# Issuing the stores of sorted weight tiles from ScalarE's queue, and splitting one row exchange into three pieces, in a fused attention and Fourier-mix kernel

## The chip, the cores and the metric

The kernel runs on one core of a Trainium2 chip. The metric is the device time of one execution in microseconds, and the time quoted for a kernel is the median of its runs. The engines named below are TensorE (PE; its weight loads are PEld), VectorE (DVE), ScalarE (ACT), GpSimd (POOL) and SyncE (SP). SP computes nothing here: it issues DMA transfers, one after the other, and before each it waits for the semaphores that the transfer depends on.

## The reference

Two blocks are fused. The first is attention with a threshold, for 8 batches of 8 heads, 576 tokens and 64 columns a head; the second mixes tokens by a two-dimensional Fourier transform and ends in a two-layer network with a normalised input. Everything is float32.

```python
scores = (1/sqrt(D)) * matmul(q, k.transpose(0, 1, 3, 2))       # (8, 8, 576, 576)
scores = where(scores >= max(scores, -1, keepdims=True) - tau, scores, -1e9)
attn   = exp(scores - max(scores, -1)); attn = attn / (sum(attn, -1) + 1e-9)
x = matmul(attn, v)  ->  rearranged to (8, 576, 512)
u = x + real(fft(fft(x, axis=1), axis=2))
un = (u - mean(u)) / sqrt(var(u) + 1e-6)
out = u + relu(un @ w_ch1) @ w_ch2                              # w_ch1: 512x2048, w_ch2: 2048x512
```

## The kernel before

**Tiling.** Attention is done for two heads at a time (a pair, number `n`), four pairs a batch, 32 pairs in all. A pair takes five steps `t` of 128 query rows (the fifth takes the last 64 rows of both heads), so there are 160 steps, numbered `i`. In the loop from L1764 one iteration of `i` holds: the scores of step `i` (`scores`, L439), the maximum (L518, DVE), the exponential (L524, ACT) and the threshold (L528, ACT) in `softmax_first`; mask and sum (L539, DVE), the reciprocal (L546, DVE) in `softmax_second`; the division (L552, ACT, two instructions for the two heads) in `softmax_third`; and, one step behind, the transposition of the finished weights of step `i - 1`, because the product with V (`values_in_parts`, L730, PE) needs keys on the partitions.

**Two ways to transpose.** In most steps PE transposes the weights (L633, L641) and ACT copies them to `et_all`. In 40 steps, eight in each of the batches 3 to 7 (counted from 0), `decide` (L571) sends them another way: DVE transposes 32x32 blocks of `e` into a buffer `et_room` (L601, in `blocks`), SP stores that buffer to DRAM (L602, `e_blocks`, 576 KB), and in a later iteration SP loads it back in four pieces so that the blocks land in their places in `et_all` (L611, `fetch`). There is a single `et_room`, in an unused part of the first weight matrix, so a transposition must wait until the store of the one before it has landed. There are three buffers `e_blocks` in DRAM.

**The network beside it.** Groups of 512 tokens go through the two-layer network as a generator that yields after every block of matmuls; `fill()` takes as many blocks from it as an evenly spread budget allows and puts them between the pieces of an attention step. From the second group on (`two_level`) products are formed by a scheme with fewer multiplications: first-stage blocks at L1288 (PE), whose results are copied by ACT (L1297 to L1306) or added by DVE (L1225) and passed through Relu by ACT (L1230), then second-stage blocks at L1437 (PE). The first stage is the `phase[0] == 1` in which `decide` chooses DVE for the transposition. The coefficients of both stages come from DRAM through a ring of five buffers (`ensure`, L1161, SP), four loads ahead.

**Folding rows.** After the last value product of a pair, `fold_rows` adds and subtracts mirrored halves of its result `x` (L792, L797; POOL for all but the last pair of a batch). Pairs of odd number need the first rows of their two heads exchanged first: `swap_rows` copies the two rows to a small tile `swap` (L759, two DMAs) and back to each other's place (L763, two DMAs, which wait for the first two). For the first pair of a batch, `x` was held in another buffer, so `fold_rows` first copies it (L779, POOL) and then calls `swap_rows`. `fold_rows` is a generator, too: a piece of it runs at each call of `fold_more`, that is at `t > 2` in the loop and at the `background()` calls in the network's blocks; what is left at step `t == 1` of the next pair is run there at once.

**Order.** The program's order on each engine is that in which the Python code emits the instructions. SP's queue therefore holds, in one line: the loads of q, k (L140) and v (L158, L161), the ring's loads (L1161), the row exchanges, the stores of `e_blocks`, the loads of `et_all` and the stores of the result (L984). ACT issues five DMAs at the very start and none afterwards.

Of the kernel before, what the change touches and what calls it, by code (L numbers as in the profile page):

```python
# [18 lines left out]
def _reversed(ap):  # L19

    n = ap.shape[1]
    return bass.AP(
        tensor=ap.tensor,
        offset=ap.offset + n - 1,
        ap=[list(ap.ap[0]), [-1, n]],
    )
# [11 lines left out]
def _stepped(ap, start, step, n):  # L38

    return bass.AP(  # L40
        tensor=ap.tensor,
        offset=ap.offset + start,
        ap=[list(ap.ap[0]), [step, n]],
    )
# [3 lines left out]
def kernel(  # L48
# [12 lines left out]
    nc = tc.nc  # L61
# [112 lines left out]
    for u in range(2):  # L174
# [14 lines left out]
        out=q_scale[:], in0=tau_t[:], scalar1=0.0, scalar2=SCALE, op0=ALU.is_ge, op1=ALU.mult  # L189
# [3 lines left out]
        out=below[:], in0=tau_t[:], scalar1=0.0, scalar2=-3.0e38, op0=ALU.is_lt, op1=ALU.mult  # L193
# [3 lines left out]
        out=tau_pos[:], in0=tau_t[:], scalar1=0.0, scalar2=-1.0, op0=ALU.max, op1=ALU.mult  # L197
# [71 lines left out]
    et_room = w1[2][:, HID // 2 : HID // 2 + 4 * 9 * 32]  # L269
# [159 lines left out]
    def scores(i):  # L429
        n, t = divmod(i, NT)  # L430
        qT, kT = heads[n][0:2]

        nh = 2 if t < 4 else 1
        sc = [ps.tile([128, 2, 512], FP32, tag="sc", name=f"sc{j}") for j in range(nh)]
        if t < 4:
            for c in range(2):
                for j in range(2):
                    hp, k0 = slice(64 * j, 64 * j + 64), D * (1 - j)
                    nc.tensor.matmul(  # L439
                        sc[j][:, c, 0:HALF], qT[hp, 128 * t : 128 * t + 128],  # L440
                        kT[hp, k0 + HALF * c : k0 + HALF * (c + 1)], start=True, stop=True,
                    )
        else:
            for c in range(2):
                nc.tensor.matmul(
                    sc[0][:, c, 0:HALF], q_ends[:, :], kT[:, D + HALF * c : D + HALF * (c + 1)],
                    start=True, stop=True,
                )
        steps[i] = (sc, nh)
# [99 lines left out]
    def softmax_third(i):  # L549
        nh, e, den = steps[i]  # L550
        for j in range(nh):
            nc.scalar.activation(  # L552
                out=e[:, S * j : S * (j + 1)], in_=e[:, S * j : S * (j + 1)], func=ACT.Copy,
                scale=den[:, j : j + 1],
            )
        if nh == 1:
            nc.scalar.copy(e[:, S : S + 64], e[:, 512:S])
        steps[i] = (e, None)

    by_dma = {}  # L560
# [32 lines left out]
    scratch = [dram.tile([128, SLOT], FP32, name=f"e_blocks{u}") for u in range(3)]  # L593

    def blocks(i):

        if not by_dma[i]:
            return
        e = steps.pop(i)[0]
        out_ = et_room.rearrange("p (b c q) -> p c b q", b=4, c=NC9)  # L600
        nc.vector.transpose(out_, e[:, 0 : 2 * S])  # L601
        nc.sync.dma_start(out=scratch[i % 3][:, :], in_=et_room)  # L602

    def fetch(i):

# [146 lines left out]
    def swap_rows(n, later=False):  # L752
        b, p = n // NPAIR, PAIRS[n % NPAIR]
        x = xs[b][p]
        if p % 2:

            swap = sb.tile([2, S], FP32, tag="half", bufs=1, name="swap")
            for j in range(2):
                nc.sync.dma_start(out=swap[j : j + 1, :], in_=x[64 * j : 64 * j + 1, :])  # L759

            def back():
                for j in range(2):
                    nc.sync.dma_start(out=x[64 * j : 64 * j + 1, :], in_=swap[1 - j : 2 - j, :])  # L763

            if late and later:
                swaps.append(back)
            else:
                back()

# [4 lines left out]
    def fold_rows(n):  # L774
        b, p = n // NPAIR, PAIRS[n % NPAIR]
        if late and n % NPAIR == 0:
            assert not mixes
            x = sb.tile([128, S], FP32, tag=f"x{p}", bufs=1, name=f"x{p}")
            nc.gpsimd.tensor_copy(x[:, :], xs[b][p][:, :])  # L779
            xs[b][p] = x  # L780
            swap_rows(n)
            yield
        x = xs[b][p]

        half = sb.tile([128, 2, HALF], FP32, tag="half", bufs=1, name="half")
        up, down = x[:, 1:HALF], _reversed(x[:, HALF + 1 : S])
        mid = S // 4

        last = n % NPAIR == NPAIR - 1
        eng = nc.vector if last else nc.gpsimd  # L790
        for c, op in enumerate((ALU.add, ALU.subtract)):
            eng.tensor_tensor(out=half[:, c, 1:HALF], in0=up, in1=down, op=op)  # L792
        yield
        for c, c0, op in (
            (0, 0, ALU.add), (0, 161, ALU.subtract), (1, FW, ALU.subtract), (1, FW + 161, ALU.add)
        ):
            eng.tensor_tensor(  # L797
                out=f[:, p, c0 : c0 + mid - 1], in0=half[:, c, 1:mid],
                in1=_reversed(half[:, c, mid + 1 : HALF]), op=op,
            )  # L800
            if late and last and c0 > 0 and c0 != FW:
                yield

        eng.tensor_tensor(
            out=f[:, p, mid - 1 : mid + 1], in0=_stepped(x, mid, -mid, 2),
            in1=_stepped(x, 3 * mid, -mid, 2), op=ALU.add,
        )
        eng.tensor_tensor(
            out=_stepped(f[:, p, :], 160, FW, 2), in0=_stepped(x, 0, mid, 2),
            in1=_stepped(x, HALF, mid, 2), op=ALU.subtract,  # L810
        )
        yield


        if n % NPAIR == 1 and b != 1:
            fold_halves(b)

    def fold_halves(b):
        sums[b] = sb.tile([128, 2, 2 * FW], FP32, tag="tmp", bufs=1, name="sums")
        fold_chunks(nc.gpsimd, b, 1)  # L820
# [692 lines left out]
    late = []  # L1513
# [28 lines left out]
    total = B * per_batch  # L1542
# [117 lines left out]
    def fold_more():  # L1660
        if folds and next(folds[0], True):
            folds.pop(0)
# [101 lines left out]
    for i in range(2 * per_batch, total + 3):  # L1764


        n, t = divmod(i, NT)
        values = iter(())
        if i < total:
            scores(i)  # L1770
        late_values = None
        if t == 3 and i < total and not by_dma.get(i - 2):
            values = values_in_parts(n, 0)
        elif t == 0 and by_dma.get(i - 4):
            values = values_in_parts(n - 1, 0)
        elif t == 1 and n > 0:
            while folds:
                fold_more()
            values = values_in_parts(n - 1, 1)
            if by_dma.get(i - 3):  # L1780
                values, late_values = iter(()), values
        next(values, None)
        if i < total:
            softmax_first(i)
        next(values, None)
        if t == 0 and by_dma.get(i - 4):
            fetch(i - 3)
        if t != 4 or not by_dma.get(i - 3):
            fetch(i - 2)
        if i % per_batch == 2:  # L1790
            for _ in last_fold:
                pass
            start_batch(i // per_batch - 1)
        fill(True)
        for _ in late_values or ():
            pass
        if i < total:
            softmax_second(i)
        while held:
            held.pop(0)()  # L1800
        decide(i - 1)
        blocks(i - 1)
        while swaps:
            swaps.pop(0)()
        if mixes:
            mix(1)
        if t == 1:
            if n % NPAIR:
                folds.append(fold_rows(n - 1))
            else:  # L1810
                last_fold = fold_rows(n - 1)
                next(last_fold)
        weights = weights_in_parts(i - 1) if i <= total else iter(())
        next(weights, None)
        if t > 2:
            fold_more()
        fill()
        if i % per_batch == 1:
            next(last_fold)
        next(weights, None)  # L1820
        if i < total:
            softmax_third(i)
            if t == 1:
                prep_ends(n)
            if t == 2 and n + 1 < B * NPAIR:
                scale_q(n + 1)
            if t == 3 and n + 1 < B * NPAIR:
                prep_pair(n + 1)
        if wanted:
            wanted.pop().factors()  # L1830
        if i % per_batch == 1:
            next(last_fold)
        fill()
        if t == 2 and n + 1 < B * NPAIR:
            load_v(n + 1)
        if t < 2 and n + 1 < B * NPAIR and len(loaded.get(n + 1, ())) == t:
            load_raw(n + 1, slice(t, t + 1))
# [50 lines left out]
```

## Time and profile before

| | us |
|---|---|
| median of 3 runs (lowest to highest) | 1633.84 (1628.51 to 1636.37) |
| the profiled execution | 1636.11 |
| its span in the trace | 1634.0 |
| PE busy | 1523.9 (93%) |
| DVE busy | 1130.0 (69%) |
| ACT busy | 904.9 (55%) |
| POOL busy | 813.3 (50%) |

A profile shows one execution. Busy time counts instructions of an engine, not its waiting for semaphores nor the issuing of DMAs. The list of waits puts each idle stretch down to the instruction or transfer whose end came last before it. In timelines a row holds the start and the time of one instruction or of several alike, and in square brackets the idle time of the engine before it with what ended it; "SPq" rows are DMA issues, whose time is that of the issue alone, not of the transfer.

### The profile page before, as it was taken

The page shows a single profiled execution, that of the slowest core. Times are in us where ns is not written, and L with a number is a line of the kernel's source. Part 1 is how long each engine was busy: PE and PEld are TensorE (multiplying, and loading weights), DVE is VectorE, ACT ScalarE, POOL GpSimd, SP SyncE. Part 2 cuts the span into 40 slices and gives each one's busy share as a digit, 9 for nine tenths or more (in the row PEclk, how much of TensorE's full clock was granted, in tenths as well). Part 3 has the DMA queues.
Part 4 walks back from the last instruction along what each step waited for, and adds up shares of the span by engine and source line. Part 5 has one row for each costly group of instructions (what it writes and reads, how often), then busy time and mean ns, then how long its engine had stood idle before and what let it go on. Part 6 is the DMA issues. An engine that isn't in the chain of part 4 may idle for free.

```text
span 1634.0 us, 27080 instructions
## 1 busy us (share of the span) xinstructions
PE 1523.9 (93%) x9410; PEld 1166.9 (71%) x9410; DVE 1130.0 (69%) x2137; ACT 904.9 (55%) x1913; POOL 813.3 (50%) x1002
## 2 busy tenths in 40 slices
PE   8998989999999989998999899998999899999997
PEld 4555545556787867876787677776787678889987
DVE  7997786846769567766677577856677666636537
ACT  5775565545666556655666566665566566233231
POOL 6784663034454623536253724553264625547646
PEclk9999999999999999999999999999999999999998
DMA  7423221645945389737975588628974696556755
GB/s 159 125 56 113 74 74 36 190 144 177 285 149 165 94 253 261 203 97 203 248 203 143 141 252 244 187 79 230 255 205 127 178 264 203 186 160 230 238 188 191
DMA packets 296253, 286.26 MB, mean 175 GB/s; under 512 B 202643, under 2 KB 241045, under 8 KB 295222
## 3 DMA queue, kind: packets, MB, share of 16 engines
q1 hardware_dynamic: 293606, 284.23, 60.6%
q8 instruction: 76, 1.25, 0.3%
q10 hardware_dynamic: 2512, 0.30, 0.2%
q14 instruction: 59, 0.48, 0.1%
HBM read 231.10 MB, written 53.22 MB: 174 GB/s over the span
## 4 chain that ended last, share of the span: by engine, by line
PE 60%; DVE 19%; DMA 6%; ACT 6%; issue 4%; POOL 2%; SPq 2%; DVEq 0%; ACTq 0%; POOLq 0%
PE ph L1288 16%; PE po L1437 15%; PE pv L730 8%; PE sc L439 6%; PE po L1015 4%; PE ph L991 2%; DMA v_in<-in_v_dram 2%; PE pw L641 2%; DVE e L479 2%; PE py L864 2%; DMA w<-f 2%; PE pw L694 2%; ACT e L524 1%; DVE e L539 1%; DVE neg L518 1%
## 5 line engine op out<-in xcount | busy, mean ns | idle before, releaser
L518 DVE TENSOR_REDUCE neg<-sc 128x1 f32<-128x576 f32 x216 | 153.8, 749 | 127.0 <-PE sc L439 117.0
L524 ACT ACTIVATE e<-sc,neg 128x576 f32<-128x576 f32 x216 | 158.4, 733 | 136.5 <-DVE neg L518 135.8
L1437 PE MATMUL po<-w,w_all 128*128 128x128 f32 x1792 | 229.6, 278 | 1.2 <-ACT et_all L634 0.8
L1437 PEld LDWEIGHTS po<-w,w_all 128*128 128x128 f32 x1792 | 214.6, 193 | 11.0 <-issue 6.2
L1234 POOL TENSOR_TENSOR w<-hs 128x512 f32<-128x512 f32 x32 | 42.1, 1318 | 352.0 <-ACT hs L1230 325.3
L539 DVE SCALAR_TENSOR_TENSOR e<-sc,thr,e 128x576 f32<-128x576 f32 x216 | 168.4, 813 | 47.4 <-ACT thr L528 47.4
L1288 PE MATMUL ph<-w_all,w 128*128 128x256 f32 x672 | 168.9, 401 | 33.4 <-DVE hs L1225 33.4
L1288 PE MATMUL ph<-u_t,w 128*128 128x256 f32 x768 | 183.1, 383 | 0.0
L439 PE MATMUL sc<-kT,qT 64*128 64x288 f32 x1024 | 171.2, 434 | 9.4 <-DVE e L479 8.1
L1288 PEld LDWEIGHTS ph<-w_all,w 128*128 128x128 f32 x672 | 130.9, 199 | 65.1 <-POOL w_all L1337 23.6
L552 ACT ACTIVATE e<-e,den 128x576 f32<-128x576 f32 x216 | 156.8, 770 | 25.3 <-DVE den L546 24.9
L1288 PEld LDWEIGHTS ph<-u_t,w 128*128 128x128 f32 x768 | 142.3, 190 | 29.9 <-issue 9.0
L439 PEld LDWEIGHTS sc<-kT,qT 64*128 64x128 f32 x1024 | 94.2, 187 | 64.3 <-issue 35.7
L1230 ACT ACTIVATE hs<-hs 128x512 f32<-128x512 f32 x64 | 54.0, 843 | 152.6 <-DVE hs L1225 152.6
L1337 POOL TENSOR_TENSOR w_all<-w_all 128x128 f32<-128x128 f32 (+2 forms) x160 | 119.6, 765 | 33.0 <-DVE w_all L1455 22.4
L1437 PE MATMUL po<-w,hs 128*128 128x128 f32 x960 | 126.3, 279 | 0.0
L1437 PEld LDWEIGHTS po<-w,hs 128*128 128x128 f32 x960 | 117.3, 194 | 9.1 <-issue 7.7
L1225 DVE TENSOR_TENSOR hs<-ph,hs 128x512 f32<-128x512 f32 x64 | 60.5, 945 | 84.1 <-PE ph L1288 78.8
L730 PE MATMUL pv<-et_all,v_rev 128*64 128x256 f32 (+1 forms) x640 | 86.2, 416 | 4.3 <-DMA out_dram<-u 2.6
L730 PE MATMUL pv<-et_all,v_in 128*64 128x256 f32 (+1 forms) x640 | 86.4, 414 | 3.9 <-ACT e L524 1.6
L906 POOL TENSOR_TENSOR u_t<-x,tmp 128x289 f32<-128x289 f32 (+1 forms) x45 | 34.0, 756 | 105.3 <-DVE tmp L901 105.3
L471 ACT ACTIVATE e<-sc,neg 128x576 f32<-128x576 f32 x72 | 52.8, 733 | 45.3 <-DVE neg L463 45.2
(235 smaller groups left out, 3204.3 us busy)
## 6 DMA issues: line engine op xcount, KB each, us to landing
w<-f SPq DMA_DIRECT2D x304, 512.0 KB, 4.4
e_blocks<-w SPq DMA_DIRECT2D x40, 576.0 KB, 4.1
et_all<-e_blocks SPq DMA_DIRECT2D x160, 144.0 KB, 3.9
hs<-in_moe_w_ch_dram SPq DMA_DIRECT2D x23, 512.0 KB, 4.7
q_in<-in_q_dram SPq DMA_DIRECT2D x128, 72.0 KB, 4.3
out_dram<-u SPq DMA_DIRECT2D x36, 256.0 KB, 4.2
k_in<-in_k_dram SPq DMA_DIRECT2D x124, 72.0 KB, 3.9
v_in<-in_v_dram SPq DMA_DIRECT2D x64, 128.0 KB, 4.7
```

The source lines that it names most:

```text
L439: nc.tensor.matmul(sc[j][:, c, 0:HALF], qT[hp, 128 * t : 128 * t + 128], kT[hp, k0 + HALF * c : k0 + HALF * (c + 1)], start=True, stop=True,)
L518: nc.vector.tensor_reduce(out=neg[:, j : j + 1], in_=sc[j][:, :, 0:HALF], axis=AXIS_XY, op=ALU.max, negate=True,)
L524: nc.scalar.activation(out=ej, in_=sc[j][:, :, 0:HALF], func=ACT.Exp, bias=neg[:, j : j + 1], scale=1.0)
L539: nc.vector.scalar_tensor_tensor(out=ej, in0=sc[j][:, :, 0:HALF], scalar=thr[:, j : j + 1], in1=ej, op0=ALU.is_ge, op1=ALU.mult, accum_out ...
L552: nc.scalar.activation(out=e[:, S * j : S * (j + 1)], in_=e[:, S * j : S * (j + 1)], func=ACT.Copy, scale=den[:, j : j + 1],)
L730: nc.tensor.matmul(pv[64 * j : 64 * j + 64, 0:m], vt[:, 2 * c + j, :], right, start=(c == 0), stop=(c == 4), skip_group_check=True,)
L1015: nc.tensor.matmul(po[:, :], hs[:, BT * j + 128 * t : BT * j + 128 * (t + 1)], w2[j], start=(j == 0), stop=(j == NJ - 1),)
L1225: nc.vector.tensor_tensor(out=to, in0=bank, in1=to if other is None else other, op=ALU.add)
L1230: nc.scalar.activation(out=to, in_=to, func=ACT.Relu)
L1288: nc.tensor.matmul(bank[:, 256 * q : 256 * q + 256].rearrange("p (two n) -> p two n", two=2), left[:, 256 * c + 128 * q : 256 * c + 128 * ...
L1337: return lambda: eng.tensor_tensor(out=to, in0=to, in1=other, op=ALU.add)
L1437: nc.tensor.matmul(to, lefts[m][j][:, s], right_[:, 128 * s : 128 * (s + 1)], start=fresh and s == 0, stop=s == 3, skip_group_check=True,)
```

## The change

The store of `et_room` leaves `blocks` and goes to a new function `keep_blocks`, which issues it from ACT's queue. It is called later in the iteration, behind `softmax_third(i)` and ahead of the scaling of the next q. What is stored, where to and how much stays the same, and so do the loads back.

For the first pair of a batch, `fold_rows` ends a piece behind the copy, ends another behind the two DMAs to `swap`, and issues the two DMAs back in a third; the additions come in the piece after that. `swap_rows` returns its second half instead of running it in that one case.

```diff
@@ blocks
         nc.vector.transpose(out_, e[:, 0 : 2 * S])
-        nc.sync.dma_start(out=scratch[i % 3][:, :], in_=et_room)
+
+    def keep_blocks(i):
+
+        if by_dma.get(i):
+            nc.scalar.dma_start(out=scratch[i % 3][:, :], in_=et_room)
@@ swap_rows
             if late and later:
                 swaps.append(back)
+            elif late:
+                return back
             else:
                 back()
@@ fold_rows
             nc.gpsimd.tensor_copy(x[:, :], xs[b][p][:, :])
             xs[b][p] = x
-            swap_rows(n)
             yield
+            back = swap_rows(n)
+            yield
+            if back:
+                back()
+                yield
@@ the loop over i
         next(weights, None)
         if i < total:
             softmax_third(i)
+        keep_blocks(i - 1)
+        if i < total:
             if t == 1:
                 prep_ends(n)
```

## The prediction

> **What bounds the kernel now.** I read the page's busy times first, then the list of waits of the engine that is busiest, then the timelines around its longest waits.
>
> ```profile
> span 1634.0 us, 27080 instructions
> PE 1523.9 (93%) x9410; PEld 1166.9 (71%) x9410; DVE 1130.0 (69%) x2137; ACT 904.9 (55%) x1913; POOL 813.3 (50%) x1002
> ```
>
> PE is the bound: 1634.0 - 1523.9 = 110 us is all that an edit of waits could win. PE runs in program order, so idle time of PE adds to the end almost one for one. The list of waits says which of it concerns the stores:
>
> ```profile
> PE ph L1288 <- DVE hs L1225: 34.7, 14, 5.1
> DVE w L601 <- DMA e_blocks<-w: 27.8, 12, 5.5
> SPq L602 <- DVE w L601: 68.2, 20, 6.6
> SPq L759 <- POOL x L779: 27.7, 5, 5.5
> SPq L763 <- DMA swap<-x: 19.1, 16, 2.3
> SPq L611 <- DMA e_blocks<-w: 11.8, 11, 1.9
> ```
>
> (Total us, times, longest.) DVE waits 27.8 us for a store to leave `et_room`; behind that DVE is late with L1225, and PE waits for L1225. The timelines of SP, DVE and PE at one such place:
>
> ```profile
> 562.45 1.17 SPq L759 DMA_DIRECT2D swap<-x  x2
> 564.81 1.19 SPq L763 DMA_DIRECT2D x<-swap  x2
> 566.05 2.19 SPq L140 DMA_DIRECT2D k_in<-in_k_dram  x4
> 568.29 0.50 SPq L1161 DMA_DIRECT2D w<-f  x1
> 568.83 0.43 SPq L602 DMA_DIRECT2D e_blocks<-w  x1
> ```
>
> ```profile
> 563.25 1.36 DVE L601 STREAM_TRANSPOSE w<-e 128x1152 f32<-128x1152 f32 x1
> ...
> 574.96 1.38 DVE L601 STREAM_TRANSPOSE w<-e 128x1152 f32<-128x1152 f32 x1 [5.27 <-DMA e_blocks<-w]
> ```
>
> ```profile
> 578.79 3.75 PE L1288 MATMUL ph<-w_all,w 128*128 128x256 f32 x8 [4.89 <-DVE hs L1225]
> ```
>
> The first tile was sorted at 564.60. SP could not store it: it stood at L759 until the copy L779 was done (562.45), then issued the exchange, four loads of k and a ring load, and came to the store at 568.83, 4.2 us late. That landed at 574.94; the next transposition, ready at 569.69, lost 5.27 us, and PE 4.89. This is the first store of a first stage, and there are five stages:
>
> | sorted | store issued | landed | DVE idle | PE idle |
> |---|---|---|---|---|
> | 564.60 | 568.83 | 574.94 | 5.27 | 4.89 |
> | 744.92 | 747.68 | 752.80 | 2.85 | 3.05 |
> | 924.02 | 928.88 | 934.07 | 5.00 | 4.60 |
> | 1101.11 | 1105.25 | 1110.71 | 4.54 | 4.15 |
> | 1280.86 | 1284.95 | 1291.37 | 5.46 | 5.07 |
>
> PE loses 21.8 us here. It loses 2.85 at 1157.82, of which 1.05 is DVE waiting for a store; its like in the other stages, where DVE doesn't wait, is 1.70 (620.65, 979.11). DVE waits 2.18 at 760.96, and PE has 1.65 just after.
>
> **What the Trainium skill says.** "Perfetto Trace Analysis", section "DMA Instruction — HWDGE": the issuing sequencer waits for a transfer's semaphores before it issues, and takes nothing else meanwhile. The trace agrees: SP stands 68.2 us at L602. Its section "Sequencer Loop": an instruction for the engine is pushed into a queue, a control instruction starts at once. So ACT's sequencer can reach a DMA ahead of the arithmetic in front of it, if that has no open wait. The trace agrees: ACT's semaphore wait for L634 first stands at 645.7, while L524, emitted before it, begins at 645.82 and again at 646.63. The HWDGE section also has a "Lock Wait" for the shared descriptor generator; no row separates it here. "DMA: Bandwidth & Descriptors", section "Issuing engines are not separate DMA queues": all transfers share 16 engines, and another issuer saves only the issuing time. Here what is saved is the queue ahead of the issue, 2.8 to 4.9 us in the table.
>
> **The store, step by step.** 40 issues leave SP (344 ns median each) and 40 join ACT; the bytes stay.
>
> *Gain, first store of a stage.* `keep_blocks` stands behind the two L552, released by the same reciprocal as the transposition (563.33), so ACT issues at the transposition's end, about 564.65. From issue to landing a store takes 3.0 / 4.1 / 6.4 us (least, median, most). With the median it lands at 568.8, before 569.69: the wait is gone. Even 5.0 us does; 6.4 leaves 1.4 of 5.27. What is then late next is DVE itself: L601, L410, L411, L413 and L1225 took 3.7 us from 574.96 to 578.64, so from 569.7 they end at 573.4, and PE is ready at 573.9. I take 21.3 of 21.8 (bounds 15 and 22), 1.0 at 1157.82 and 1.5 around 760.96 (0 to 1.05 and 0 to 2.2): **23.8**, bounds 15 and 25.
>
> *Loss, last store of a stage.* Here ACT is later than SP was:
>
> ```profile
> 641.38 0.34 SPq L602 DMA_DIRECT2D e_blocks<-w  x1
> ...
> 646.18 2.07 SPq L611 DMA_DIRECT2D et_all<-e_blocks  x4
> ```
>
> ```profile
> 643.53 1.06 ACT L1230 ACTIVATE hs<-hs 128x1024 f32<-128x1024 f32 x1 [2.75 <-DVE hs L1225]
> 644.49 1.43 ACT L552 ACTIVATE e<-e,den 128x576 f32<-128x576 f32 x2
> ```
>
> ```profile
> 652.20 2.38 PE L730 MATMUL pv<-et_all,v_in 128*64 128x256 f32 x20 [0.72 <-DMA et_all<-e_blocks]
> ```
>
> ACT's sequencer waits for L1225 until 643.5, then passes L1230 and L552: store at 643.6, 2.2 us later. It lands 4.0 later, at 647.6 instead of 645.4; the loads back begin 1.4 us late, and behind them stand two ring loads and v. The ring load at 648.34 lands 654.94 for a block used at 659.17, so it bears that; the product L730 doesn't. The same at 825.34, 1003.97, 1183.62 and 1359.39 makes the loads 1.6 to 2.2 us late; part returns, as the k loads ahead of them have drained by then (loads back took 4.6 us at 1359.39 without k loads, 5.7 to 7.5 with them), and the last has 2.4 us of slack. I take 4 x 1.1 = **4.5** (0 to 11; 11 if the store is issued only when L552 ends, at 645.95).
>
> *Loss, ACT's time.* In the first stage ACT is closed up from L552 (563.45) to L524, and DVE waits for its threshold. The issue ends at about 565.0 where L397 began at 564.79: 0.25 us, in ten such iterations, of which five have no slack (the 1.70 gaps). With the lock I allow 0.4: 5 x 0.4 = **2.0** (1 to 6; SP's slowest issues here take 1.3 to 1.6). Elsewhere ACT idles behind the issue (2.1 to 7.4 us before L1230). At `t = 4` the store moves 1.2 us later; the load back there comes 1 to 6 us after the landing: nothing, or 1 us if that cover goes.
>
> **The exchange in pieces.** Nothing is added but two yields, six times. SP no longer stands at L759 for POOL (5 us, five times) or at L763. With the store off SP nothing PE needs waits behind these: ring loads have at least 4 us of slack, and k is needed from 576. The additions come two pieces later on POOL; they ended at 574.6, and the next pair's exchange, which needs their buffer, comes at 600.1. If it bunches up before `t = 1`, POOL waits some 3.6 us for the two exchanges; POOL is 50% busy. I take 0 (-2 to +3).
>
> **Sum.** 23.8 - 4.5 - 2.0 = 17.3 us. The profiled execution took 1636.11 (span 1634.0 and 2.1 around it), so its like would take 1618.8; against the median 1633.84, that is 2.3 lower, the forecast is **1616.5**. What a measurement of this kernel can tell from no change is about 0.5%, 8.2 us.
>
> **Rivals.**
> 1. *The late store eats the gain.* If ACT issues only when L552 has ended, the last stores are 4.5 us later and cost 11, those at `t = 4` 2.9 later (1 more), and ACT's time 2 to 4: 23.8 - 11 - 1 - 4 = 8, **1626**. For it: L552 ends at 645.92. Against: L634's early wait. Chance 0.17.
> 2. *The landing stays late.* The store now shares the DMA engines with what SP issues at the same time; at 575 to 579 these are full. If it lands 6.4 us after the issue, residual waits of 1.4 x 5, with 4.5 and 6 lost: 23.8 - 7 - 10.5 = 6, **1627.5**. Against: the k loads would already be through. Chance 0.08.
> 3. *ACT becomes the bound (slower).* Each store holds ACT's sequencer until DVE has finished, then for the descriptor generator while SP uses it, with exponentials queued behind. If a store delays ACT by d on PE's path in all 40 places, the sum is 23.8 - 4.5 - 40 d: no gain from d = 0.48 us, over 0.5% slower from 0.7. At 0.9 it is +17: **1650**. For it: closed-up ACT at 563 to 569. Against: SP's issues of it took 0.32 to 0.53, and after 20 of the 40 ACT idles. Chance 0.09.
> 4. *The change doesn't do what it says* for the exchange: if the pieces are all run together at `t = 1`, SP waits as before. It costs nothing against my sum.
>
> **Numbers.** The first case has 0.66: 1616.5, from 1608.5 (nothing lost, 25 won) to about 1624. Rivals 1 and 2 lie around the bound and are split between faster and same; the third is mostly slower. Faster 0.74, same 0.15, slower 0.11. The range 1607 to 1630 leaves the third case out and a little below.
>
> **What would show it.** Right: 40 issues of `e_blocks` on ACTq; DVE's wait for them under 6 us; PE's for L1225 from 34.7 to about 12; no SPq row L602 <- DVE; SPq L611 <- e_blocks up from 11.8 towards 20; L730 waiting 1 to 2 us at the ends of stages. Wrong: DVE still waiting over 3 us at the first stores; ACT rows beginning over 0.5 us later behind the store; or PE's new waits at L730 adding up to over 11.

## The result, and the profile after

| | before | after |
|---|---|---|
| median (lowest to highest, 4 runs) | 1635.11 (1628.51 to 1638.97) | 1658.51 (1655.39 to 1660.90) |
| the profiled execution, its span | 1636.11, 1634.0 | 1660.90, 1659.1 |

The change makes the kernel slower: the ratio is 1.0146 (95% interval 1.0108 to 1.0184), some 24 us, where 1616.5 us were forecast.

The page of after: PE has no more work than before, but 5.7 us more of busy time, and the value product L734 has become dear.

```profile
span 1659.1 us, 27069 instructions
...
PE 1529.6 (92%) x9410; PEld 1166.8 (70%) x9410; DVE 1138.9 (69%) x2137; ACT 907.0 (55%) x1913; POOL 817.8 (49%) x1002
...
L734 PE MATMUL pv<-et_all,v_in 128*64 128x256 f32 (+1 forms) x640 | 106.5, 488 | 41.5 <-DMA et_all<-e_blocks 17.4
...
e_blocks<-w ACTq DMA_DIRECT2D x40, 576.0 KB, 3.7
```

Last number of the third row: PE idled 41.5 us ahead of L734; before it was 3.9. The list of waits of after (total us, times, longest; L1298 is the old L1288, L1235 the old L1225, L1240 the old L1230, L734 the old L730, L615 the old L611, L1171 the old L1161, and L606 the store, formerly L602):

```profile
DVE w L601 <- DMA e_blocks<-w: 6.3, 6, 2.3
PE ph L1298 <- DVE hs L1235: 12.8, 11, 1.7
PE pv L734 <- DMA et_all<-e_blocks: 17.4, 8, 3.7
PE pv L734 <- DMA w<-f: 12.4, 4, 4.9
SPq L615 <- DMA e_blocks<-w: 52.8, 16, 5.6
SPq L1171 <- DMA e_blocks<-w: 43.1, 5, 9.4
SPq L161 <- DMA e_blocks<-w: 9.3, 4, 3.0
```

The first two rows are the forecast gain, and it came: PE's gaps at the first store of the five stages went from 4.89, 3.05, 4.60, 4.15 and 5.07 us to 0.15, 1.19, 0.14, 0.14 and 0.14. The last two rows are the surprise. A ring load of coefficients (L1171) and a load of v (L161) have nothing to do with a sorted tile, and yet SP stood for its store, up to 9.4 us at a time. SP's timeline in the second pair of the first stage:

```profile
599.90 8.14 SPq L615 DMA_DIRECT2D et_all<-e_blocks  x4
...
611.26 4.82 SPq L615 DMA_DIRECT2D et_all<-e_blocks  x4
616.18 10.10 SPq L1171 DMA_DIRECT2D w<-f  x3
626.38 5.11 SPq L615 DMA_DIRECT2D et_all<-e_blocks  x8
```

Four issues of a load back took 2.07 us before; here the first four take 8.14, since the third of them stood from 602.16 to 607.26. ACT's timeline says for what:

```profile
604.46 0.33 ACTq L606 DMA_DIRECT2D e_blocks<-w  x1
...
620.34 1.06 ACT L1240 ACTIVATE hs<-hs 128x1024 f32<-128x1024 f32 x1 [4.78 <-DVE hs L1235]
...
622.31 0.33 ACTq L606 DMA_DIRECT2D e_blocks<-w  x1
```

The store of 604.46, of the *next* tile, landed at 607.24, and SP went on. The store of 622.31 landed at 625.39; from 616.57 to 625.41 SP had stood for it at a ring load. The trace's semaphore numbers give the reason: in this program every DMA that SP or ACT issues signals one of eight completion semaphores (100, 102, 103, 105 to 109), dealt out in turn over both queues when the program is built, and most of them (903 of 1076 here) first wait for that semaphore, that is, until the DMA that had it before has landed. The third piece of the load back and the store of 604.46 both have 103; the ring load and the store of 622.31 have 100. While all stores stood in SP's own order, the earlier user of a semaphore was also earlier in the queue. Now it can be a store that ACT will issue later: set against SP's order in experiment 2 (the later place, on SP), the next SP transfer with a store's semaphore stands three transfers ahead of the store's place for the fifth store of each stage, and one ahead for the seventh. PE pays behind SP:

```profile
572.91 1.96 PE L1298 MATMUL ph<-w_all,w 128*128 128x256 f32 x8 [0.15 <-DVE hs L1235]
...
620.39 4.04 PE L734 MATMUL pv<-et_all,v_in 128*64 128x256 f32 x20 [1.98 <-DMA w<-f]
...
636.50 4.60 PE L734 MATMUL pv<-et_all,v_in 128*64 128x320 f32 x20 [3.05 <-DMA et_all<-e_blocks]
```

The second row is put down to a ring load, but the last piece of the load back that the product needs had landed only at 620.15. The twenty matmuls of 256 columns took 2.38 us where PE had not idled (577.71), 4.04 here; those of 320 columns took 2.91 before (637.33), 4.60 here: a gap costs more than its idle time.

### The profile page after: what moved, and what is told of

The parts are those of the page before. It is cut to its first block, busy times and chain, and to the rows that moved or that the text cites. A ratio compares the mean times of both kernels' runs of the same rounds, so it can differ in the third digit from the quotient of the medians.

```text
span 1659.1 us, 27069 instructions
## 1 busy us (share of the span) xinstructions
PE 1529.6 (92%) x9410; PEld 1166.8 (70%) x9410; DVE 1138.9 (69%) x2137; ACT 907.0 (55%) x1913; POOL 817.8 (49%) x1002
## 4 chain that ended last, share of the span: by engine, by line
PE 55%; DVE 19%; DMA 11%; ACT 7%; issue 4%; POOL 2%; SPq 1%; ACTq 0%; DVEq 0%; POOLq 0%
PE po L1447 14%; PE ph L1298 13%; PE pv L734 8%; PE sc L439 5%; PE po L1025 4%; DMA et_all<-e_blocks 3%; DMA w<-f 3%; DMA e_blocks<-w 2%; PE ph L1001 2%; ACT e L524 2%; DVE e L479 2%; PE pw L645 2%; DVE e L539 2%; PE pw L698 2%; PE py L874 2%
## 5 line engine op out<-in xcount | busy, mean ns | idle before, releaser
L524 ACT ACTIVATE e<-sc,neg 128x576 f32<-128x576 f32 x216 | 158.6, 734 | 132.3 <-DVE neg L518 131.5
L1298 PE MATMUL ph<-u_t,w 128*128 128x256 f32 x768 | 183.0, 383 | 0.0
L1298 PE MATMUL ph<-w_all,w 128*128 128x256 f32 x672 | 159.4, 384 | 12.0 <-DVE hs L1235 11.6
L1298 PEld LDWEIGHTS ph<-u_t,w 128*128 128x128 f32 x768 | 142.4, 190 | 29.8 <-issue 8.2
L1298 PEld LDWEIGHTS ph<-w_all,w 128*128 128x128 f32 x672 | 125.1, 190 | 42.8 <-issue 13.6
L734 PE MATMUL pv<-et_all,v_in 128*64 128x256 f32 (+1 forms) x640 | 106.5, 488 | 41.5 <-DMA et_all<-e_blocks 17.4
L1235 DVE TENSOR_TENSOR hs<-ph,hs 128x512 f32<-128x512 f32 x64 | 60.5, 945 | 119.5 <-PE ph L1298 114.3
L1240 ACT ACTIVATE hs<-hs 128x512 f32<-128x512 f32 x64 | 54.0, 843 | 135.0 <-DVE hs L1235 135.0
L734 PEld LDWEIGHTS pv<-et_all,v_in 128*64 128x64 f32 x640 | 55.8, 163 | 88.5 <-issue 52.1
L734 PE MATMUL pv<-et_all,v_rev 128*64 128x256 f32 (+1 forms) x640 | 84.7, 411 | 7.3 <-DMA out_dram<-u 4.7
```

The source lines that it names most:

```text
L524: nc.scalar.activation(out=ej, in_=sc[j][:, :, 0:HALF], func=ACT.Exp, bias=neg[:, j : j + 1], scale=1.0)
L734: nc.tensor.matmul(pv[64 * j : 64 * j + 64, 0:m], vt[:, 2 * c + j, :], right, start=(c == 0), stop=(c == 4), skip_group_check=True,)
L1235: nc.vector.tensor_tensor(out=to, in0=bank, in1=to if other is None else other, op=ALU.add)
L1240: nc.scalar.activation(out=to, in_=to, func=ACT.Relu)
L1298: nc.tensor.matmul(bank[:, 256 * q : 256 * q + 256].rearrange("p (two n) -> p two n", two=2), left[:, 256 * c + 128 * q : 256 * c + 128 * ...
```

## The experiments

All times are medians, with the ratio to the kernel before on the same chip (in brackets its 95% interval); the experiments ran on several chips, and the kernel before took 1630.09 to 1635.11 us on them, so where runs of two chips are compared, the ratios are the better measure. Line numbers shift by a few from kernel to kernel. Theory A is the shared semaphores. Theory B: ACT's queue or the later place in the program is what loses. Theory C: the split exchange loses.

**1. Each part alone.** `e1_store_only` leaves `fold_rows` and `swap_rows` as before; `e2_swap_only` leaves the store in `blocks` on SP.

> Only the store goes to ACT; the row exchange stays in one piece. Theory A (the completion semaphores that SP and ACT take in turn make SP wait for the landing of ACT's stores, and what SP issues behind, the loads back above all, comes late): 1650 to 1665 us, with SP's waits for e_blocks<-w over 70 us in sum again. Theory B (only the place on ACT is late): about the same, 1650 to 1665. Theory C (the split exchange is what costs): 1612 to 1625, the time forecast for the whole change.

> Only the row exchange is split; the store stays on SP behind the transposition. On SP the exchange now stands behind the first store of a stage, so the store no longer waits for the copy on POOL. Theories A and B: DVE's wait for the first stores (21 us in five stages) goes, and nothing on ACT or in the turn of semaphores changes: 1606 to 1618 us, SP's waits for e_blocks<-w at most 15 us. Theory C: 1650 or more.

Measured: the store alone 1666.43 us, ratio 1.0195 (1.0157 to 1.0232), just above the range of A and B, with SP's waits for `e_blocks<-w` 106.6 us in sum. The split exchange alone 1606.37, ratio 0.9827 (0.9808 to 0.9846). Theory C falls: the exchange, priced at nothing, is the gain, 27 us, and the store is the loss. SP's timeline of the split exchange alone (L602 is the store, L759 the exchange) and two rows of its list of waits:

```profile
563.62 0.34 SPq L602 DMA_DIRECT2D e_blocks<-w  x1
564.06 0.38 SPq L1167 DMA_DIRECT2D w<-f  x1
564.54 2.12 SPq L759 DMA_DIRECT2D swap<-x  x2
```

```profile
DVE w L601 <- DMA e_blocks<-w: 4.4, 5, 1.5
PE ph L1294 <- DVE hs L1231: 14.2, 9, 3.4
```

With the pieces the exchange is emitted behind the first store of the stage; the store goes out 0.03 us after the transposition that ended at 563.59, from SP. The same two waits as in after have gone, without ACT. The store alone removes them, too, and yet loses:

```profile
PE ph L1292 <- DVE hs L1229: 13.1, 13, 1.7
PE pv L734 <- DMA et_all<-e_blocks: 29.4, 12, 4.8
```

**2. The later place, but on SP.**

```diff
-            nc.scalar.dma_start(out=scratch[i % 3][:, :], in_=et_room)
+            nc.sync.dma_start(out=scratch[i % 3][:, :], in_=et_room)
```

> The whole change, but the store is issued from SP at the new, later place of the program. Theory A: SP's own order and the turn of semaphores agree again, so the waits of 5 to 9 us go: 1608 to 1625 us. Theory B (the later place in the program is what costs): 1645 or more.

Measured: 1642.47, ratio 1.0046 (1.0025 to 1.0066), between the two. The waits of L615 for a store fell to 18.2 us, as A says, but the later place has a price of its own on SP, where the second half of an exchange and a ring load now stand ahead of the store (tile sorted at 569.08, stored at 572.37):

```profile
DVE w L601 <- DMA e_blocks<-w: 42.3, 16, 5.5
PE ph L1298 <- DVE hs L1235: 22.8, 9, 5.1
```

So this run does not decide between A and B.

**3. The early place, on ACT.** `keep_blocks(i - 1)` right behind `blocks(i - 1)`.

> The whole change, but ACT issues the store right behind the transposition, ahead of the division and of what is emitted between. Theory A: the semaphores are still shared by the two queues, so 1645 to 1665 us and SP's waits for e_blocks<-w still over 50 us. Theory B (place on ACT): the last stores of a stage come up to 7 us earlier and the loss goes: 1612 to 1630.

Measured: 1654.98, ratio 1.0125 (1.0100 to 1.0149). It differs from `e2_swap_only` in the issuing queue alone, and the store is issued 0.03 us behind every transposition, so the lateness of the store is not the cause. Waits and timelines of SP and PE:

```profile
SPq L615 <- DMA e_blocks<-w: 53.8, 16, 6.3
SPq L158 <- DMA e_blocks<-w: 30.3, 5, 7.1
PE pv L734 <- DMA et_all<-e_blocks: 24.0, 7, 6.0
ACT hs L1307 <- DVE w L601: 29.3, 11, 3.0
```

```profile
601.49 8.55 SPq L615 DMA_DIRECT2D et_all<-e_blocks  x4
```

```profile
626.75 4.53 PE L734 MATMUL pv<-et_all,v_in 128*64 128x256 f32 x20 [4.84 <-DMA et_all<-e_blocks]
```

The last row of waits is a second cost: at the early place ACT itself stands until the transposition ends, with the copies L1307 and L1311 behind.

**4. POOL's queue.** As in 3 with `nc.gpsimd.dma_start`.

> As the one with the early store on ACT, but POOL issues the 40 stores, whose completion semaphores are not among the eight of SP and ACT. Theory A (SP is held by semaphores that it shares with ACT's stores): SP's waits for a store that it does not load back go; 1606 to 1630 us, where the upper part is for stores that stand behind additions on POOL. Theory B (any queue but SP's loses, since loads and stores of a tile then stand in two queues): 1645 or more.

Measured: 1640.19, ratio 1.0047 (1.0031 to 1.0064): above A's range. POOL's stores use other semaphores (111 to 118), and SP no longer waits for a store at L158, L161 or the ring loads, as A says; but stores stand behind additions on POOL (first store of the first stage 3.09 us late) and several landed after 6 to 9 us, so SP waits 62.7 us at the loads back, which do need the store, and DVE waits again:

```profile
DVE w L601 <- DMA e_blocks<-w: 33.2, 15, 4.8
PE ph L1298 <- DVE hs L1235: 30.8, 14, 5.9
```

It takes SP's foreign waits away and puts another loss there, so it is no clean test either.

**5. The turn of semaphores put right, first try.** In the program of experiment 3, by the semaphore numbers of the trace set against SP's order with the split exchange alone, the next user of a store's semaphore stands three, six and three transfers *ahead* of the store's old place, for three of the eight stores of a stage. A 64-byte write by SP into the same buffer, on which the store then depends, moves the store behind SP's transfers when semaphores are dealt out; in both kernels below it is never ahead.

```diff
         if by_dma.get(i):
+            nc.sync.dma_start(out=scratch[i % 3][0:1, 0:16], in_=ones[0:1, 0:16])
             nc.scalar.dma_start(out=scratch[i % 3][:, :], in_=et_room)
```

> As the one with the early store on ACT, with one thing added: ahead of each store SP writes 64 bytes to the first row of the same e_blocks buffer, and the store waits for that. This puts the store behind SP's earlier transfers when the build deals out the semaphores, so that no SP transfer ahead of the store's old place takes the store's semaphore any more (in the version without it, three of the eight of a stage do). 40 transfers and 40 waits more. Theory A: SP's long waits go; 1606 to 1620 us in spite of the added work. Theory B (ACT's queue itself loses): 1655 or, with the added work, more.

> The whole change as it is, store at the later place on ACT, with the same 64 bytes written by SP ahead of each store. Theory A: the part of the loss that comes from shared semaphores goes, and what stays is the lateness on ACT: 1615 to 1635 us. Theory B (the later place on ACT is the cause): 1650 or more, as the change.

Measured: 1654.04, ratio 1.0111 (1.0055 to 1.0166), and 1683.12, ratio 1.0311 (1.0268 to 1.0355). Both missed A's ranges, and the second lies in B's. The list of waits of the first shows why this doesn't speak for B: PE's wait for loads back is nearly gone, but ACT stands for the 64 bytes, which SP reaches late. In the second ACT stands 39.8 us for them at L1241 alone.

```profile
PE pv L735 <- DMA et_all<-e_blocks: 1.8, 2, 1.2
PE ph L1299 <- ACT hs L1312: 26.1, 5, 7.2
ACT hs L1312 <- DMA e_blocks<-ones: 26.7, 4, 7.9
```

The test had replaced the wait by another one.

**6. The same write, early.** It is now emitted right behind `scores(i)`, to land before the tile is sorted. The first store of each stage goes without it: 35 writes in all.

```diff
+    def mark(i):
+        n, t = divmod(i, NT)
+        if i < B * NPAIR * NT and in_blocks(n) and t < 4 and phase[0] == 1:
+            nc.sync.dma_start(out=scratch[i % 3][0:1, 0:16], in_=ones[0:1, 0:16])
...
             scores(i)
+        mark(i - 1)
```

> As the one with the early store on ACT, but SP writes its 64 bytes right behind the scores of the iteration, ahead of the loads back, so that they have landed before the tile is sorted and ACT does not stand for them. By the order in which the build deals out the semaphores, no SP transfer that belongs ahead of a store takes that store's semaphore. Theory A: the 5 us waits of PE for the loads back in the second pair go (some 35 of the 49 us that the early store on ACT lost against the store on SP); what stays is ACT held by the wait for the transposition, some 14: 1615 to 1628 us. Theory B (ACT's queue or place as such): 1650 or more.

> The whole change with the same early 64 bytes written by SP. Theory A: SP's waits of 5 and 9 us for stores of later tiles go; what stays is the later place, with the last store of a stage 7 to 10 us behind its transposition: 1618 to 1640 us. Theory B (the later place on ACT causes the whole loss): 1655 or more.

> Only the row exchange split, store on SP, and the same early 64 bytes: what the added writes cost by themselves. Both theories: 1604 to 1614 us.

| kernel | without the write | with it (ratio, interval) |
|---|---|---|
| split exchange, store on SP | 1606.37 | 1602.62 (0.9818, 0.9793 to 0.9843) |
| split exchange, store early on ACT | 1654.98 | 1615.60 (0.9900, 0.9872 to 0.9927) |
| the change: store later on ACT | 1658.51 | 1626.91 (0.9967, 0.9953 to 0.9981) |

Thirty-five transfers more make both kernels with the store on ACT faster, by 39 and 32 us in medians and by 37 and 29 by the ratios, and move the one with the store on SP by nothing that its interval tells (its 1602.62 is a little under the range expected). With the write no SP transfer that takes a store's semaphore next stands ahead of that store's old place. Waits and timelines of SP and PE in the second kernel of the table (L621 is the load back):

```profile
SPq L158 <- DMA e_blocks<-w: 30.7, 5, 7.4
SPq L621 <- DMA e_blocks<-w: 12.7, 13, 4.3
PE pv L740 <- DMA et_all<-e_blocks: 2.3, 2, 1.2
PE ph L1304 <- ACT hs L1317: 9.3, 5, 2.1
```

```profile
598.18 1.75 SPq L621 DMA_DIRECT2D et_all<-e_blocks  x4
...
609.37 0.38 SPq L158 DMA_DIRECT2D v_in<-in_v_dram  x1
...
610.85 1.75 SPq L621 DMA_DIRECT2D et_all<-e_blocks  x4
```

```profile
617.93 2.38 PE L740 MATMUL pv<-et_all,v_in 128*64 128x256 f32 x20
```

The load back goes out in 1.75 us instead of 8.55, and the product has no gap. SP still stands 30.7 us for stores at L158, as in experiment 3, and PE hardly pays for it: of the two loads back that the product needs the first (598.18) is already ahead of that place, and the second (610.85) stands behind it but has landed by 617.10, just before PE comes to the product. In experiment 3 the first was held until 609.24, the second went out only from 618.78, and its last piece was held by one more store until 624.05. So it is not the foreign wait as such, but how late it leaves what stands behind it. This shows theory A: stores at the same place of the same queue (0.03 us behind the transposition in 3, and at most 1.15 here), another deal of semaphores, 37 to 39 us.

What is left of B is the difference to the store on SP, 13 us at the early place and 24 at the later one. At the early place the last row of waits above shows a part of it, which fits ACT's stand for the transposition (23.1 us in sum at L1313 and L1317): L1317 is late, and PE waits 9.3 us for it. At the later one (the profiled execution, 1634.01, is the slowest of sixteen):

```profile
DVE w L601 <- DMA e_blocks<-w: 9.7, 8, 2.2
PE ph L1304 <- DVE hs L1241: 20.5, 10, 4.0
PE pv L740 <- DMA et_all<-e_blocks: 8.5, 4, 2.8
```

**7. The prediction's sum for the store alone.** Experiment 1's store with the early 64 bytes, exchange in one piece.

> Only the store goes to ACT, exchange in one piece, and SP writes the early 64 bytes, so that the semaphores are dealt out in an order that holds SP up little. This is the prediction's sum for the store alone, with its missing term taken out: 1617 us if the rest of the sum was right (23.8 won at the first stores, 6.5 lost). If the later place on ACT costs what it cost with the split exchange (24 us against the store on SP), about as before: 1630 to 1640.

Measured: 1642.81, ratio 1.0074 (1.0046 to 1.0102), above both ranges. The write brings 24 us against the store alone without it (20 by the ratios), and PE's wait for loads back falls from 29.4 to 8.4 us, as with another deal of semaphores. But the kernel stays slower than before: the rest of the sum doesn't come out here. SP stands 27.7 us for POOL's copy as before, and ACT now 17.1 us for the 64 bytes (ACT hs L1240 <- DMA e_blocks<-ones), so a part of this loss is the test's own, and how large it is stays open.

## Why the prediction was wrong, point by point

- **The bound, and the wait that goes.** Right, nearly to the number. DVE's wait for a store was to fall under 6 us and is 6.3; PE's for L1225 to about 12 and is 12.8. At the first stores PE idles 20.0 us less (21.3 forecast).
- **To whom the gain belongs.** Wrong. The 23.8 us were credited to the store, and the exchange was taken at 0 (-2 to +3). The exchange alone brings 27 us, with the store left on SP. The prediction had the cause in hand (SP stood at L759 for POOL and came 4.2 us late to the store), but asked of the split only who waits for the exchange, after the store had been moved away, and not where the exchange would then stand against a store that stays. Two edits removed the same wait, and either does it alone (PE's wait for DVE is 14.2 us with the exchange alone, 13.1 with the store alone). So what each is worth depends on the other: on top of the store on ACT the exchange brings 8 us by the medians (1666.43 against 1658.51), where the intervals of the ratios overlap; with the early write it brings 16 (1642.81 against 1626.91), in part the wait that the test itself put in.
- **The failed step.** "40 issues leave SP (344 ns median each) and 40 join ACT; the bytes stay." The sum asked what stands behind a store on ACT, and not who waits for the store's semaphore on SP. That term, absent, is 32 us at this place by the medians (1658.51 against 1626.91), 29 by the ratios. The prediction rested here on the Trainium skill, "DMA: Bandwidth & Descriptors", section "Issuing engines are not separate DMA queues", by which another issuer saves only the time of issuing; the runs show that in this program it can also cost. "Perfetto Trace Analysis", section "DMA Instruction — HWDGE", by which a sequencer waits for a transfer's semaphores before it issues, was the other half, and the trace agrees with up to 9.4 us at L1171. A hint stood in the list of waits of before: SP waits 3.6 us in 11 places at L140, a load of q or k, for loads back that it has nothing to do with.
- **Last store of a stage, 4.5 us (0 to 11).** Its size failed with the step above. The store was to be issued 2.3 us behind the transposition; in after it is 7.2 to 10.8, because the product behind the late load back is late, ACT's copies L740 and L741 wait for it, and the store stands behind those. With the early write it is 2.4 to 3.0 us at the ends of the five stages, so the reading of when ACT would issue was right. Yet all that remains of the later place is 24 us, not 6.5 (4.5 and 2.0), so these terms were too small as well. What the trace shows of it: PE's wait at L1304 for DVE, where DVE waits for a store that lands late, is 3.48 to 4.02 us in four of the five second pairs (1.70 was usual), and at the ends of four stages PE idles 1.97 to 2.81. How the 24 us divide between ACT's queue and the later place stays open.
- **The rivals.** The first, a late store that eats the gain, has its mechanism in the trace, as a consequence. The second, a late landing, is a part of what remains: in the kernel of experiment 6 with the later place a store issued at 602.21 let DVE go on only at 609.30. The third, ACT as the bound, is not seen; ACT's arithmetic was held for the transposition only at the early place. The fourth, pieces run together, did not happen: with the exchange split, SP's 27.7 us at it for POOL's copy are gone. No rival had the mechanism that decided.
- **What was to show it wrong** did: new waits at the value product of over 11 us (41.5 ahead of L734, 3.9 before).
- **Idle time was counted one for one.** A gap of PE costs more. The prediction's own line showed it: the eight matmuls behind the gap at 578.79 took 3.75 us, the same eight without a gap in after (572.91) 1.96. In experiment 3 the stretch from the start of the scores at 620.67 to the end of the product at 631.28 is 10.6 us; with the store on SP it is 3.56. Of the 7.05 us between them 4.84 are idle and 2.15 are slower matmuls. It holds for the gain as well: with the split exchange alone the span is 28.7 us shorter than before, of which 18.2 are idle time of PE (91.9 against 110.1) and 10.5 busy time (1513.4 against 1523.9), at a mean granted clock of 0.981 instead of 0.973. By idle time alone the exchange would have been taken for two thirds of what it brings.

One way from before to after, in runs: exchange and 64 bytes with the store on SP -29, later place on ACT +24, semaphores +28 to +32 (against the kernel before, or medians directly): some +24. These are steps of one chain, so they add up by construction; in another order the steps differ, as the exchange shows. The fastest kernel here keeps the second part of the change alone: 1602.62 with the 64 bytes, 1606.37 without, which the intervals don't separate.

## What to carry to other kernels

Where two edits aim at one wait, price each with the other undone: here the cheap reordering of the queue had the whole gain, and the move to another queue added only its own costs. Before a DMA changes its queue, look in the list of waits for issues that wait for transfers they don't use. In this program they came from completion semaphores that two queues share, and a transfer on the queue that ran behind held the one that ran ahead. What such a wait costs is decided by what stands behind it. Where a wait of PE is priced, look also at how long the matmuls behind it take.

## What the runs showed of the hardware

- Matmuls start slowly after a gap. Behind the 1.98 us gap at 620.39 in after, pairs of matmuls of 256 columns (the two start within 0.04 us) started 427 ns apart for 3.4 us, and then 216 ns; the granted clock is 0.50 from 620.39 to 623.80 and 1.00 in the 3.4 us before and the 6.2 us behind. Behind the 4.84 us gap of experiment 3 it is 0.50 for 5.95 us. The Trainium skill, "TensorE: Matmul & The Clock Gate", section "Part 1: The HAM clock gate", says that the array's clock is halved after an idle window of about 3.4 us and comes back after a busy one; the traces agree with the factor, and in the first case with the time of return, and show that a gap of 2 us was enough here (PE was busy 1.41 of the 3.39 us before 620.39). In after the products with `v_in` (L734) took 20 us more of PE's busy time than before (106.5 against 86.4).
- A store of 576 KB by POOL occupied POOL for 0.57 us at its issue (median; at most 0.77); on ACT and SP an issue took 0.33 and 0.34 (medians).
- The stores that SP and ACT issued signalled semaphores of one set of eight (100, 102, 103, 105 to 109), those of POOL another (111 to 118).
